# Mirrored weight rows gathered ahead of x instead of behind its first tiles, with the first layer's schedule ranked anew

## The chip, the cores and the metric

The kernel runs on one core of one Trainium2 chip. The metric is the device time of one execution in microseconds (us), the median of three runs. In the text PE is TensorE, ACT is ScalarE, DVE is VectorE, POOL is GpSimd, and SP is SyncE, which here only issues DMA transfers. The core has 16 DMA engines. Tiles of x are counted from t = 0 to 15; each holds 128 rows of 448 numbers.

## The reference

Two layers, each a spectral filter followed by a feed-forward block, on x of 2048 rows by 448 columns in bf16. The reference, cut to what is computed:

```python
def _A_ref(x, w_r, w_i):                 # spectral filter
    X = jnp.fft.rfft2(x.astype(jnp.float32), axes=(-2, -1))
    X = X * (w_r + 1j * w_i)             # w_r, w_i: 2048 x 225
    return jnp.fft.irfft2(X, s=(S, D), axes=(-2, -1)).astype(jnp.bfloat16)

def _B_ref(x, w1, b1, w2, b2):           # feed-forward, 448 -> 1792 -> 448
    h = jnp.einsum("bsd,df->bsf", x, w1) + b1
    r = jnp.where(h > 0, h, 0)
    return jnp.einsum("bsf,fd->bsd", r * r, w2) + b2

x = A_x
x = x + _A_ref(_layernorm(x), A_w_r, A_w_i)
x = x + _B_ref(_layernorm(x), B_w1, B_b1, B_w2, B_b2)
x = x + _A_ref(_layernorm(x), A_w_r, A_w_i)     # the same weights again
x = x + _B_ref(_layernorm(x), B_w1, B_b1, B_w2, B_b2)
```

## The kernel before

The Fourier transforms are matmuls with constant matrices. The stages of the first layer, in order: A1 (layer-norm statistics of each x tile, then 5 matmuls per tile against the matrix FA scaled by the tile's 1/sigma, then an eviction to XA), TD (matmuls with TD_sb), B (with G_sb), W (the product with the weights, on DVE), Bi (with H_sb), TI and AI (the way back, and the sum with x), then the feed-forward block. The second layer has the same stages with A2 in place of A1.

The W stage needs the weights in two SBUF tiles, Wa and Wb, which lie in the memory of `xin` and `yT` (the profile uses these names). Both hold rows of w_r and w_i in straight order, and the same rows once more in mirrored order. The straight rows are plain loads. For the mirrored rows of Wa, POOL issues two indirect DMA transfers (one for w_r, one for w_i), each of which gathers 64 rows of 3600 numbers by the row numbers in `back`. The mirrored rows of Wb are copied from Wa by SP, from SBUF to SBUF. Two further copies put the mirrored rows into DRAM (`Wrev`), from which the second layer reloads them.

All instructions are recorded first; a list scheduler in the kernel then orders them on each engine by a rank (`PR`, one number for each group of work) and may choose the engine of some of them from a set (`EN`). Each engine then runs its instructions in that order and waits on semaphores. The start of the recorded program:

```python
back = sb("back", [64, 1], mybir.dt.int32)
sch.add("pool", lambda e: e.iota(back[:], [[0, 1]], base=127, channel_multiplier=-2), [], [back[:]], cost=100.0)
memset(warm[:, 0:1], 1.0)
memset(epst[:, 0:1], EPS)
act(warm[:, 0:1], warm[:, 0:1], ACT.Sqrt)
sch.chain = {}                              # from here on each issuing engine keeps its DMA order
dma("act", FA_sb[:], dc["FA"])
dma("act", b1r, B_b1.rearrange("(f p) -> f p", p=P))
dma("act", J_sb[:], dc["J"])                # reversed identity
for e, a, b in (("sp", 0, 2), ("sp", 2, 4), ("sp", 4, 8), ("sp", 8, 12), ("sp", 12, 16)):
    dma(e, x_sb[:, a:b, :], x_dram[:, a:b, :], slow=1.5)
for i in range(2):                          # the gathers: they read back AND a piece of x
    o = Wa[1 - i::2, 17 * WC + 1:33 * WC + 1]
    src = A_w_i if i else A_w_r
    sch.add("pool", lambda e, o=o, src=src: e.indirect_dma_start(
        o, None, src.rearrange("(q k) l -> q (k l)", k=16), bass.IndirectOffsetOnAxis(back[:, 0:1], 0)),
        [back[:], x_sb[:, 1, 0:2]], [o], is_dma=True, cost=1200.0, lat=2.0 * 64 * 16 * WC / sch.DMA_RATE)
# ... memset of ones and of Z (on POOL)
for a, b in ((0, 2), (2, 4), (4, 6), (6, 8), (8, 10), (10, 12), (12, 14), (14, 16)):
    at[:] = 0, a // 2
    evac(xr[:, a:b, :], x_sb[:, a:b, D - 1:HD - 1:-1], "A1x")    # mirrored half of two x tiles
dma("sp", TD_sb[:], dc["TD"])

def load_W(W, f, p0, p1, first):
    # ... straight rows of w_r and w_i into W, two plain loads on SP
    for i in range(2):
        # ...
        if not first:
            dma("sp", o, Wrev[i][...], reads=[f"Wrev{i}"])       # second layer: from DRAM
        elif f:
            dma("sp", o, Wa[1 - i::2, c0:c1], slow=1.3)          # Wb: SBUF copy from Wa

for n, (p0, p1) in enumerate(RANGES):
    dma("sp", G_sb[...], dc["G"][...])
    load_W(Wa, 0, p0, p1, True)
    load_W(Wb, 1, p0, p1, True)
    dma("sp", H_sb[...], dc["H"][...])
for i in range(2):
    dma("sp", Wrev[i], Wa[1 - i::2, 17 * WC + 1:33 * WC + 1], writes=[f"Wrev{i}"])
# ...
def b1_columns():                           # bias b1 turned into columns: one matmul with J_sb
    q = _Tile(1)
    mm(q[lambda b: ps[:, b, 0:FB]], b1r, J_sb[0:FB, P - FB:P][:, ::-1], True, True)
    cp(b1T[:, 0:FB], q[lambda b: ps[:, b, 0:FB]])               # on DVE
# ...
for q in range(8):                          # stage A1
    ln_stats([2 * q, 2 * q + 1], True)      # BN_STATS on DVE; for t = 1, 3, 11 sums on ACT
    ln_rstd([2 * q, 2 * q + 1])
    first_A(2 * q)                          # scale FA into Fs, 5 matmuls, eviction to XA
    first_A(2 * q + 1)
b1_columns()
spectral(True)
ffn(False)
```

Where PE would be idle the scheduler puts matmuls on a tile of ones whose result nobody reads (line 1157, `ps<-ones`); they keep the array busy.

Of the kernel before, what the change touches and what calls it, by code (L numbers as in the profile page):

```python
# [25 lines left out]
WC = 225  # L26
# [85 lines left out]

PR = {'TD': [[1510607, 1492741, 1491034, 1343318, 1393964, -3615858, 1398823, 973064, 1485741], [2520683, -882130, 2513278, 1403817, -946609, -1006157, -1079382, -1083072, 1408461]], 'B': [[1485140, 1514860, 1501477, 1399358, 1504936, -3591466, 1503956, -3590078, 961566], [2513805, -1004943, 1405526, 2514030, 1385417, -1091018, 967616, -1128168, -974908]], 'W': [[1849139, 1836802, 1884322, 1860165, 1860418, 981529, 1855478, 1880484, 986484], [258958, 196705, -32086, -31831, 199273, -68617, -58145, -231565, -289839]], 'Bi': [[992350, -3627728, -3593143, -3606899, -3606153, -3597099, -3606581, -3605094, -3596021], [-1103789, 969189, -981009, 1254540, 970491, 1105225, 1552262, 1255862, 1105109]], 'ln': [[991126, 1016681, 13698, -12192, 3592, -9275, 58717, 59319, 60173], [-215928, -161644, -233516, -1278285, -1243220, -1249248, -1270637, -1075997, -1090994]], 'TI': [[4661211, 3603451, 3461865, -3320802, 3581733, -3314912, 3577378, -3303437, -3557233], [1148985, 1261825, -1055731, -1010406, -1074609, -1083367, -1026469, -1043258, -1050048]], 'AI': [[3603697, 4997207, 4997530, 4979074, 3482668, 4986081, 4943161, 4901552, 4992029], [-1080862, 1269571, 943460, -1102619, 1036527, 1203915, -1142225, 1214879, 1183541]], 'xb': [[966, 109389, -75965, -110358, -218149, -39133, -137679, -133462, -146632], [-874934, -227306, -1248899, -1550879, -1543334, -1550645, -1548009, -1575947, -1598280]], 'h': [[4994138, 5003910, 4900585, 4903100, 4901125, 4954442, 5002645], [-1085930, 1201108, 1202903, 1171062, 1082119, 1231856, 1056057]], 'o': [[5025464, 5043598, 4946662, 4825629, 4947511, 4769147, 4931712, 4939797, 4905816, 4965852, 4907640, 4758088, 4928290, 3664542, 4936102, 3571000], [1035960, 1041613, 1046935, 1054242, 1080488, 1155787, 1169102, 1155870, 1000585, 1239792, 1159813, 1159789, 1170072, 1159974, 1163403, 1047019]], 'A2': [[-34871, -450185, -573944, -145705, 153605, 80879, -602905, 81580, 79768, -84049, 81902, 81224, 99503, 452346, 464311, 452106]], 'A1': [[1811154, 1811355, 1842735, 1845662, 1842065, 1842576, 1826448, 1840939]], 'aux': [[1505401, -292702, -154625, 1848161]], 'A1x': [[1811802, 1797921, 1830263, 1787522, 1758506, 1787869, 1798665, 1812907]], 'A1f': [[1815437, 1814986, 1840060, 1843242, 1984370, 1791775, 1844072, 74669]], 'A1m': [[1502233, 1479272, 1517675, 1507165, 1503516, 1518961, 1518966, 1489731]], 'A1e': [[928729, 1815500, 1902353, 928717, 1675923, 1716716, 1675936, 1943634]], 'A2f': [[-34049, -127990, -606838, -439476, -138011, 89305, -571804, 80322, 86631, 80269, 450792, 462862, 54580, 466206, 59337, 450170]], 'A2s': [[480058, 130187, 326278, 591247, -431528, 73495, -83424, -22736, -590315, -851545, -746374, -585928, -115865, -441429, 129400, 466571]], 'A2m': [[4922555, 4746350, 4716000, 4727107, 4938752, 4935914, 4721112, 4719912, 3545281, -1102588, 3449906, 3544553, -1101765, 4721131, 3545586, -1101726]], 'A2e': [[43630, 40194, -682618, -204383, 162475, -55941, 457346, -202207, 210383, 251692, -640306, -43305, -207937, 110571, 278833, 493288]], 'TDe': [[954306, 1843647, 965927, 1000070, 978035, 876912, 1001412, 997131, 1721659], [234287, 1417255, 495995, 497071, -692296, -708408, 116793, 481473, -31496]], 'Be': [[1746203, 1001954, 1683907, 960405, 1780546, 967818, 1669193, 1684490, 963029], [-673471, -562228, -700927, 509333, -668554, 482845, -571588, -638456, -610624]], 'Ws': [[1889039, 1798939, 1854874, 1886651, 814650, 911035, 1938936, 1878593, 1822359], [212971, -52164, -46639, -245211, -58995, -232137, -245502, -184844, -32998]], 'Bie': [[971134, 947163, 1784532, 1001939, 1002073, 987816, 1001937, 1001943, 1001461], [1425225, 487576, -647465, -980124, -655085, -74395, -74265, -181695, -980116]], 'TIe': [[913909, 919877, 722393, -268012, 716509, -288603, 853646, 1008636, 792915], [-149289, -168051, -87569, -1092127, -1364282, -1052619, -148265, -1019412, -75009]], 'AIf': [[-308433, 3579, -182406, 12653, 80551, 7729, -143107, -148725, -142263], [-1045428, -423729, -1430802, -276728, -1103758, -1170272, -918535, -1355679, -1095738]], 'AIs': [[1037824, 921138, 43475, 988, 25617, -29947, -110980, 57417, 53976], [-160854, -145123, -793906, -883581, -1371555, -217899, -1046764, -1245627, -1325531]], 'lnq': [[254432, -546412, 123603, 7472, -193124, -186442, 9410, 836140, -149412], [-287651, -1394001, -1546005, -1125253, -1199492, -1202077, -101648, -1538229, -1522243]], 'lny': [[168910, 899305, 37852, 73400, -12667, 102790, 55869, -23759, 84279], [-244523, -464919, -208553, -1628453, -1450315, -1200119, -1077933, -1545496, -1133605]], 'fl': [[4991518, -3553909, 5045833, 5074410, 3443910, -3419830, 4794596, -3248326, 4963895], [-1100203, -1109390, -1282316, -1178605, -1592271, -1453810, 732254, -1093079, -1088719]], 'fle': [[-189687, 766990, -622264, 878315, -707948, 922239, -284319, -762173, -301700], [-1435726, -776655, -779325, -884711, -359745, -150713, -909732, -337434, -263372]], 'hA': [[-173623, -61538, 82981, 166072, -461795, 94451, 17384], [-59738, -1239374, -1219139, -169082, -1225583, -1223164, -59731]], 'hD': [[24938, -128082, -607193, -606364, -517680, 4299, -81566], [-949150, -1571960, -1533320, -1506174, -1592396, -1567483, -1293058]], 'oD': [[6213, -23599, -603373, -443574, 151235, 130944, 83824, 118459, -119914, 133726, 132035, -4922, 78773, 479772, 77491, 442182], [-1549288, -1077336, -1522386, -1421216, -1499943, -906811, -859800, -1465910, -1534119, -1026687, -1633193, -1551677, -1535519, -1571610, -1461819, -1620002]]}
EN = {'lny': ['addbdbadb', 'aadbdadbb'], 'A1x': ['brxprrdr'], 'A1f': ['xrpxprbp'], 'A1e': ['abbbbaab'], 'A2s': ['dbbabbabadbbbddb'], 'A2e': ['abaabababdaadbaa'], 'TDe': ['adbbababb', 'abadaaaad'], 'Be': ['bbbabbbaa', 'abaaabaaa'], 'Bie': ['baaaadaab', 'aaaaabbda'], 'TIe': ['adbbbbaaa', 'aabdabbbb'], 'fle': ['badababdb', 'bddaabaab']}
ENG = {"a": ("act",), "d": ("dve",), "p": ("pool",), "b": ("act", "dve"), "q": ("act", "pool"), "r": ("dve", "pool"),
       "x": ("act", "dve", "pool")}
LOOK = {"act": 0.0, "dve": 50.0, "pe": 0.0}
# [386 lines left out]
def bass_interleave_layers__spectral_gfnet__dense_activation_squared_relu__prompt_kernel(nc, A_x, A_w_r, A_w_i, B_x, B_w1, B_b1, B_w2, B_b2, out):  # L506
# [4 lines left out]
    sch = _Sched()  # L511

    with ExitStack() as es:
# [8 lines left out]
        x_sb = x_raw[:, 0:NT * D].rearrange("p (t d) -> p t d", t=NT)  # L522
# [7 lines left out]
        xb = arena[:, 2 * FB * 512:2 * FB * 512 + NT * D].rearrange("p (t d) -> p t d", t=NT)  # L530
# [7 lines left out]
        Wa = xin[:].rearrange("p t d -> p (t d)")[:, 0:33 * WC + 1]  # L538
# [76 lines left out]
        def rank(k, L=None, n=None):  # L615
            if L is not None:
                at[:] = L, n
            sch.bias = PR[k][at[0]][at[1]]

        def evac(o, i, key):  # L620
            engs = ENG[EN[key][at[0]][at[1]]]
            rank(key)
# [35 lines left out]
        def memset(o, v, eng="dve"):  # L658
            sch.add(eng, lambda e: e.memset(o, v), [], [o], cost=_free(o) / 1.92 + 60.0)  # L659
# [6 lines left out]
        out_dram = out.rearrange("b (p t) d -> p (b t) d", t=NT)  # L666
        back = sb("back", [64, 1], mybir.dt.int32)
        sch.add("pool", lambda e: e.iota(back[:], [[0, 1]], base=127, channel_multiplier=-2), [], [back[:]], cost=100.0)
        memset(warm[:, 0:1], 1.0)
        memset(epst[:, 0:1], EPS)  # L670
        act(warm[:, 0:1], warm[:, 0:1], ACT.Sqrt)
# [3 lines left out]
        dma("act", J_sb[:], dc["J"])  # L675
        for e, a, b in (("sp", 0, 2), ("sp", 2, 4), ("sp", 4, 8), ("sp", 8, 12), ("sp", 12, 16)):
            dma(e, x_sb[:, a:b, :], x_dram[:, a:b, :], slow=1.5)
        for i in range(2):
            o = Wa[1 - i::2, 17 * WC + 1:33 * WC + 1]
            src = A_w_i if i else A_w_r  # L680
            sch.add("pool", lambda e, o=o, src=src: e.indirect_dma_start(
                o, None, src.rearrange("(q k) l -> q (k l)", k=16), bass.IndirectOffsetOnAxis(back[:, 0:1], 0)),
                [back[:], x_sb[:, 1, 0:2]], [o], is_dma=True, cost=1200.0, lat=2.0 * 64 * 16 * WC / sch.DMA_RATE)
        w_dram = [w.rearrange("(q k) l -> q (k l)", k=32) for w in (A_w_r, A_w_i)]
        Wrev = nc.dram_tensor("Wrev", (2, 64, 16 * WC), BF16, kind="Internal").ap()
        memset(ones[:], 1.0)
# [554 lines left out]
```

## Time and profile before

| what | value |
|---|---|
| time, median of 3 runs | 270.92 us (270.76 to 271.03) |
| span of the profiled execution | 269.0 us |
| PE busy | 257.3 us (96%), of it 17.1 us in 54 matmuls on ones |
| DVE, ACT, POOL busy | 202.7, 184.6, 11.0 us |
| DMA | 23.25 MB; of it 0.92 MB in the POOL queue (the gathers) |
| granted TensorE clock, mean | 1.000 |

The page of the profile has a row of digits for each engine, one for each fortieth of the span (6.7 us), which is the busy share in tenths. Its chain of work follows back from the last instruction to whatever released each one, and so names what the end hung on. The lists of waits say which engine sat idle until what. A DMA instruction in the timeline shows only its issue; the time to landing is listed apart.

### The profile page before, as it was taken

The page shows a single profiled execution, that of the slowest core. Times are in us where ns is not written, and L with a number is a line of the kernel's source. Part 1 is how long each engine was busy: PE and PEld are TensorE (multiplying, and loading weights), DVE is VectorE, ACT ScalarE, POOL GpSimd, SP SyncE. Part 2 cuts the span into 40 slices and gives each one's busy share as a digit, 9 for nine tenths or more (in the row PEclk, how much of TensorE's full clock was granted, in tenths as well). Part 3 has the DMA queues.
Part 4 walks back from the last instruction along what each step waited for, and adds up shares of the span by engine and source line. Part 5 has one row for each costly group of instructions (what it writes and reads, how often), then busy time and mean ns, then how long its engine had stood idle before and what let it go on. Part 6 is the DMA issues. An engine that isn't in the chain of part 4 may idle for free.

```text
span 269.0 us, 6410 instructions
## 1 busy us (share of the span) xinstructions
PE 257.3 (96%) x2383; PEld 163.9 (61%) x2383; DVE 202.7 (75%) x704; ACT 184.6 (69%) x392; POOL 11.0 (4%) x24
## 2 busy tenths in 40 slices
PE   4899999999999999999999999998999999999996
PEld 1477997785755554444567986776754544554454
DVE  0784998999999998556599899799899855213622
ACT  4397997995889368783387998877989785005700
POOL 4361000000000000000000000000000000000000
PEclk9999999999999999999999999999999999999999
DMA  6999990003733730004000000002056200010011
GB/s 195 407 347 369 356 340 8 0 2 92 137 130 98 131 125 0 2 0 141 0 2 0 2 1 2 4 0 41 20 109 132 47 0 20 34 53 19 0 37 51
DMA packets 24474, 23.25 MB, mean 86 GB/s; under 512 B 16284, under 2 KB 20988, under 8 KB 24316
## 3 DMA queue, kind: packets, MB, share of 16 engines
q1 hardware_dynamic: 23968, 21.82, 27.3%
q0 software_dynamic: 160, 0.92, 0.8%
q8 instruction: 19, 0.31, 0.5%
q10 hardware_dynamic: 316, 0.10, 0.2%
q14 instruction: 11, 0.09, 0.1%
HBM read 15.49 MB, written 2.76 MB: 68 GB/s over the span
## 4 chain that ended last, share of the span: by engine, by line
PE 79%; ACT 10%; DVE 5%; DMA 4%; issue 1%; ACTq 0%
PE ps L588 77%; ACT XA L628 3%; ACT arena L628 3%; DMA J_sb<-c_J 2%; DMA yT<-xin 2%; PE ps L1157 2%; ACT tmp L628 1%; DVE arena L646 1%; ACT mv L611 1%; DVE x_raw L936 1%; DVE st L966 1%; ACT VT L628 1%; DVE tmp L629 0%; ACTq L583 0%; DVE x_raw L938 0%
## 5 line engine op out<-in xcount | busy, mean ns | idle before, releaser
L611 ACT ACTIVATE arena<-ps,b1T 128x512 bf16<-128x512 f32 (+1 forms) x140 | 74.0, 614 | 31.2 <-PE ps L588 30.9
L588 PE MATMUL ps<-yT,W_sb 64*128 64x512 bf16 (+1 forms) x980 | 87.1, 333 | 1.0 <-DMA yT<-xin 0.7
L588 PE MATMUL ps<-W_sb,arena 128*128 128x448 bf16 (+1 forms) x476 | 86.8, 342 | 0.0
L588 PEld LDWEIGHTS ps<-yT,W_sb 64*128 64x128 bf16 x980 | 50.3, 94 | 37.3 <-ACT arena L611 5.1
L588 PEld LDWEIGHTS ps<-W_sb,arena 128*128 128x128 bf16 x476 | 46.1, 98 | 37.8 <-DVE arena L646 0.8
L646 DVE TENSOR_TENSOR arena<-arena 128x512 bf16<-128x512 bf16 (+1 forms) x140 | 47.9, 367 | 19.1 <-ACT arena L611 18.7
L1055 DVE TENSOR_TENSOR x_raw<-ps,arena 128x448 bf16<-128x448 f32 (+1 forms) x23 | 13.3, 579 | 20.8 <-PE ps L588 20.8
L628 ACT ACTIVATE arena<-ps 128x896 bf16<-128x896 f32 (+1 forms) x32 | 25.6, 905 | 2.5 <-PE ps L588 2.5
L1157 PE MATMUL ps<-ones 128*128 128x512 bf16 x54 | 17.1, 440 | 1.1 <-DVE ones L659 1.1
L628 ACT ACTIVATE VT<-ps 128x512 bf16<-128x512 f32 x28 | 16.2, 680 | 2.7 <-PE ps L588 2.7
L628 ACT ACTIVATE XA<-ps 128x512 bf16<-128x512 f32 x30 | 16.3, 595 | 2.6 <-PE ps L588 2.4
L646 DVE TENSOR_TENSOR arena<-tmp 128x896 bf16<-128x896 bf16 (+1 forms) x32 | 17.1, 591 | 0.3
L738 ACT ACTIVATE tmp<-x_raw 128x448 bf16<-128x448 bf16 x14 | 8.0, 574 | 13.4 <-DVE x_raw L1051 13.3
L588 PE MATMUL ps<-H_sb,arena 128*128 128x128 bf16 x256 | 16.5, 219 | 0.5 <-DVE arena L646 0.5
L738 ACT ACTIVATE VT<-x_raw 128x448 bf16<-128x448 bf16 x24 | 13.8, 582 | 4.3 <-DVE x_raw L938 4.3
L588 PEld LDWEIGHTS ps<-H_sb,arena 128*128 128x128 bf16 x256 | 14.8, 98 | 2.5 <-DVE arena L646 2.5
L646 DVE TENSOR_TENSOR tmp<-VT 128x224 bf16<-128x224 bf16 (+1 forms) x56 | 16.2, 318 | 0.2
L938 DVE SCALAR_TENSOR_TENSOR x_raw<-ps,x_raw 128x448 bf16<-128x448 f32 x24 | 14.3, 616 | 0.8 <-PE ps L588 0.8
L588 PE MATMUL ps<-arena,G_sb 128*128 128x224 bf16 x128 | 14.3, 259 | 0.1
L628 ACT ACTIVATE tmp<-ps 128x896 bf16<-128x896 f32 (+1 forms) x16 | 12.7, 853 | 1.9 <-PE ps L588 1.9
L611 ACT ACTIVATE mv<-mv,epst 128x2 f32<-128x2 f32 (+1 forms) x31 | 9.1, 300 | 5.6 <-DVE mv L752 4.4
L588 PEld LDWEIGHTS ps<-arena,G_sb 128*128 128x128 bf16 x128 | 11.9, 98 | 0.7 <-ACT arena L628 0.6
(77 smaller groups left out, 266.2 us busy)
## 6 DMA issues: line engine op xcount, KB each, us to landing
W_sb<-in_B_w_dram SPq DMA_DIRECT2D x2, 896.0 KB, 6.5
out_dram<-x_raw SPq DMA_DIRECT2D x15, 112.0 KB, 1.7
W_sb<-in_B_w_dram SPq DMA_DIRECT2D x1, 1568.0 KB, 12.7
x_raw<-in_A_x_dram SPq DMA_DIRECT2D x3, 448.0 KB, 6.2
H_sb<-c_H SPq DMA_DIRECT2D x1, 1088.0 KB, 9.3
yT<-xin SPq DMA_DIRECT2D x4, 225.0 KB, 5.3
Wrev<-xin SPq DMA_DIRECT2D x2, 450.0 KB, 10.4
xin<-Wrev SPq DMA_DIRECT2D x4, 225.0 KB, 3.8
```

The costliest lines, as they stand in the source:

```text
L588: op = sch.add("pe", lambda e: e.matmul(_res(o), lhsT, rhs, start=start, stop=stop, skip_group_check=skip), [lhsT, rhs], [o], cost=max(_fr ...
L611: sch.add("act", lambda e: e.activation(o, _res(i), func, **kw), rd, [o], cost=c)
L628: op = sch.add("act", lambda e: e.activation(o, _res(i), ACT.Copy) if h[0].eng == "act" else e.tensor_copy(o, _res(i)), [i], [o], cost=c[" ...
L646: sch.add(eng, lambda e: e.tensor_tensor(o, _res(a), b, op), [a, b], [o], cost=_free(o) / rate + 69.0)
L738: sch.add("act", lambda e: e.activation(o, x, ACT.Square, accum_out=sd[:, t, 1:2]), [x], [o, sd[:, t, 1:2]], cost=560.0)
L936: sch.add("dve", lambda e, xx=xx, xi=xi, r=r: e.tensor_tensor(xx, _res(r), xi, ALU.add), [r, xi], [xx], cost=536.0)
L938: small(lambda e, xx=xx, xi=xi, r=r, i=i: e.scalar_tensor_tensor(out=xx, in0=_res(r), scalar=1.0, in1=xi, op0=ALU.mult, op1=ALU.add, accum ...
L966: small(lambda e, i=i: e.bn_stats(st[:, i, 0:6], x_sb[:, i, 0:D]), [x_sb[:, i, 0:D]], [st[:, i, 0:6]], 536.0)
L1055: sch.add("dve", lambda e: e.tensor_tensor(o, _res(i), xb[:, t, d0:d1], ALU.add), [i, xb[:, t, d0:d1]], [o], cost=(d1 - d0) / 0.96 + 69.0)
L1157: return lambda e: e.matmul(ps[:, b, :], ones[:], ones[:, None, :].to_broadcast([P, 4, P]), start=True, stop=True)
```

## The change

The two gathers are recorded before everything else that moves data, directly behind the `iota` that writes their row numbers, and they no longer read x. In the kernel before they named a piece of x as an input, and so waited until its first two tiles had landed. The purpose is to have the mirrored rows of Wa in SBUF sooner: SP's queue waits for them before it copies them into Wb and issues all later loads. All transfers stay the same in number, size and issuing engine.

Beside it the ranks of the first layer and the engine sets of some evictions and copies were fitted anew; those of the second layer (the second list of each entry) are unchanged. In the sets, a is ACT, d DVE, p POOL, b ACT or DVE, q ACT or POOL, r DVE or POOL, x any of the three; the letters of A1x are one for each pair of x tiles.

```diff
-PR = {'TD': [[1510607, 1492741, ... ], [2520683, -882130, ...]], ... }        # cut
-EN = {'lny': ['addbdbadb', 'aadbdadbb'], 'A1x': ['brxprrdr'], 'A1f': ['xrpxprbp'], 'A1e': ['abbbbaab'], 'A2s': ['dbbabbabadbbbddb'], ... }
+PR = {'TD': [[1288052, 1208402, ... ], [2520683, -882130, ...]], ... }        # cut
+EN = {'lny': ['dadddbbaa', 'aadbdadbb'], 'A1x': ['bxrqqbqp'], 'A1f': ['qxrpqxdp'], 'A1e': ['bbadabaa'], 'A2s': ['bbdabbbdbaadbddd'], ... }
@@ -666,6 +666,12 @@
         sch.add("pool", lambda e: e.iota(back[:], [[0, 1]], base=127, channel_multiplier=-2), [], [back[:]], cost=100.0)
+        for i in range(2):
+            o = Wa[1 - i::2, 17 * WC + 1:33 * WC + 1]
+            src = A_w_i if i else A_w_r
+            sch.add("pool", lambda e, o=o, src=src: e.indirect_dma_start(
+                o, None, src.rearrange("(q k) l -> q (k l)", k=16), bass.IndirectOffsetOnAxis(back[:, 0:1], 0)),
+                [back[:]], [o], is_dma=True, cost=1200.0, lat=2.0 * 64 * 16 * WC / sch.DMA_RATE)
         memset(warm[:, 0:1], 1.0)
@@ -675,12 +681,6 @@
             dma(e, x_sb[:, a:b, :], x_dram[:, a:b, :], slow=1.5)
-        for i in range(2):
-            o = Wa[1 - i::2, 17 * WC + 1:33 * WC + 1]
-            src = A_w_i if i else A_w_r
-            sch.add("pool", lambda e, o=o, src=src: e.indirect_dma_start(
-                o, None, src.rearrange("(q k) l -> q (k l)", k=16), bass.IndirectOffsetOnAxis(back[:, 0:1], 0)),
-                [back[:], x_sb[:, 1, 0:2]], [o], is_dma=True, cost=1200.0, lat=2.0 * 64 * 16 * WC / sch.DMA_RATE)
         w_dram = [w.rearrange("(q k) l -> q (k l)", k=32) for w in (A_w_r, A_w_i)]
```

In the built program this changes the order on the engines as follows. POOL issues both gathers right behind its memset and ahead of its first copy of x. On PE the warm-up matmuls on ones become 6, then 9 behind the bias matmul (they were 6 and 7), and 7 behind the first four tiles (they were 8). On DVE the bias copy stays the first instruction that waits. Of the 8 mirrored copies of x, DVE makes none (it made 2), ACT 2 (0), POOL 6 (6). Of the 16 scalings of FA, DVE makes 3 (5), ACT 4 (1), POOL 9 (10). Of the 16 evictions to XA, DVE makes 3 (0) and ACT 13 (16). In the first layer's TD, B and Bi stages some blocks of matmuls swap places, and so do some blocks of the second layer's A2. The order of the second layer's other matmuls is the same.

## The prediction

> **What bounds the kernel now.** I read the row of digits for the whole span first, then the chain of work that ended last in order of time, then the waits of the first 60 us, then the DMA queues slice by slice for the first 14 us. The row of PE:
>
> ```profile
> PE   4899999999999999999999999998999999999996
> ```
>
> PE stands at 9 tenths or more nearly everywhere except in the first two fortieths. The chain says the same in pieces (start, length, what):
>
> ```profile
> 1.86 5.50 DMA J_sb<-c_J
> 7.66 3.10 PE ps L1157 x7
> 10.76 2.92 PE ps L588 x15
> ...
> 21.42 2.56 ACT XA L628 x5
> 24.07 16.54 PE ps L588 x200
> ...
> 54.24 89.96 PE ps L588 x784
> ```
>
> From 24.07 us on the chain is mostly PE matmuls, and between 54.24 and 144.2 nothing else. Before 24.07 it is something else: the landing of the reversed identity J_sb at 7.36, then warm-up matmuls on ones, then stage A1, which ends with five ACT evictions to XA. So this change can act on the time through one door: the moment at which A1 ends, 24.07 us, and after it whatever the newly ranked order does. The waits of the first 60 us (who waited for what: us in total, times, longest) and, in the second fence, those of SP's queue:
>
> ```profile
> DVE b1T L650 <- PE ps L588: 6.7, 1, 6.7
> PE ps L588 <- DMA J_sb<-c_J: 3.6, 1, 3.6
> POOL xin L681 <- DMA x_raw<-in_A_x_dram: 2.7, 1, 2.7
> ```
>
> ```profile
> SPq L583 <- DMA xin<-in_A_w_r_dram,back: 4.4, 1, 4.4
> ```
>
> DVE's first real instruction is the bias copy b1T; it waits for the bias matmul, and that for J_sb. Though x[0:2] lands at about 3.6 us (ACT's first sum starts at 3.64), DVE starts its statistics only at 7.79. The last two lines are the waits that the change removes: POOL's 2.7 us for x, and SP's 4.4 us (7.2 to 11.62) for the first gather. The question is whether somebody needs what SP issues afterwards. The first user is the W stage on DVE:
>
> ```profile
> 27.23 0.39 DVE L646 TENSOR_TENSOR tmp<-arena,xin 128x448 bf16<-128x448 bf16 x1
> 27.54 0.38 DVE L646 TENSOR_TENSOR tmp<-arena,yT 128x448 bf16<-128x448 bf16 x1
> ```
>
> It starts at 27.23 directly behind the evictions of stage B, with no wait for a DMA, 12 us or more after the gathers: issued at 4.54 and 6.38, they landed after 7.1 and 6.7 us, at 11.6 and 13.1. From 27.23 to 45.8 DVE has no idle time at all. So the removed waits stand on nobody's path.
>
> **What the skill says.** The page "DMA: Bandwidth & Descriptors", section "Issuing engines are not separate DMA queues", says that transfers issued from SP, ACT and GpSimd run on the same 16 DMA engines and interleave; its section "Queues, rings and completion order" says that each engine goes round-robin between the queues that have work, one packet at a time. The trace agrees. In the slice from 9 to 10 us, with the gathers (q0) under way, the queues show
>
> ```profile
> q0 software_dynamic: 38, 0.27, 65.0%
> q1 hardware_dynamic: 83, 0.16, 42.4%
> ```
>
> (packets, MB, share of 16 engines), while SP's queue q1 had 97.8% in the slice from 7 to 8. A gather packet takes 0.65 x 16 / 38 = 0.274 us. So gathers push the loads of other queues back by what they move. The page "TensorE: Matmul & The Clock Gate", section "Part 1: The HAM clock gate", says that the array runs at half rate until it has been busy for some 3.4 us. The trace has the two rates (matmuls on ones at a pitch of 0.43 us at 8 us and of 0.22 at 14), though the change comes at about 13, some 5.4 us after PE restarted at 7.49. So a warm-up matmul is dear early and cheap later.
>
> **The change part by part.**
>
> *Removed: POOL's wait for x.* Worth nothing by itself. POOL's next needed result is a scaled FA at 11.55, behind 4.3 us of idle time.
>
> *Removed: SP's stall.* Nothing on the path, as shown. The DMA engines weren't idle during the stall either: their share was 0.97 in both slices from 5 to 15 us, since SP had queued 2.6 us of issues ahead. Only 14 to 16 us dips (0.88, 244 GB/s), worth perhaps 0.7 us of transfer, ahead of a W stage with slack.
>
> *Moved: 0.92 MB of gather traffic into the loading of x, FA and J_sb.* The first gather can be issued when POOL's memset ends, at 1.84 us, the second about 1.1 later. In the kernel before the first q0 packet appears in the slice from 8 to 9 us, at about 8.8, some 4.3 us behind the issue at 4.54. The same lag puts it at about 6.2 now. At 400 GB/s the gathers take 2.3 us of all 16 engines, so loads that are still queued at 6.2 (the last two of x, TD, G, straight rows) land up to 2.3 us later. The last piece of x was issued at 2.6 and landed 6.8 us later, at 9.4; now about 11.5. DVE reaches those tiles only at about 17 us, so that is hidden. TD_sb, issued at 3.07 with 8.1 us to landing, goes from 11.2 to 13.5 and is needed at 24. Hidden as well.
>
> *J_sb is the one load with no slack.* Its packets and those behind it in ACT's queue (q10) number 37, 66 and 41 in the slices from 4 to 5, 5 to 6 and 6 to 7 us, none later. Those after 6.2, some 33, are 2 for each engine. If each waits for one gather packet more, J_sb is 2 x 0.274 = 0.55 us late; if the first q0 packet comes at 5.2 it is 1.5 us, and if at 7, nothing. I take 0.3 us. It goes straight into the start of DVE and PE.
>
> *The new order in A1.* Three sums. First, PE has two more cold matmuls on ones behind the bias matmul: 2 x 0.43 = 0.86 us, first tile not before 11.5 (was 10.65); but now all four of the first tiles' scaled FA are made at once, so the four groups end at about 11.5 + 7 x 0.21 + 13 x 0.11 = 14.4 against 14.04, or 0.4 later. Second, ACT from its first square root behind the four evictions (14.74) to the last XA (23.97) had no idle time: 6 square roots at 0.19, two sums at 0.65, one FA at 0.4, 12 evictions at 0.53, together 9.2 us. Now it has the same roots and sums, one copy of x at 0.5, two FA at 0.8 in all and 9 evictions at 4.8: 8.5 us, 0.7 less. Third, DVE takes three evictions at about 0.65 behind its last reciprocal (21.45 before, then idle from 22.3 to 25.42): it would end them at about 23.7 + 0.3. The two engines thus end A1 at nearly the same time as before, shifted by J_sb: 24.07 + 0.3, give or take 0.8.
>
> *From 24 us on.* Number and shape of all matmuls are unchanged. PE had no gap of its own from 24.07 to 40.45 and from 54.24 to 144.2, so swapping blocks there moves nothing unless it makes a wait. The filler counts of the program behind A1 are equal (2, 5, 2, 2, 3, 3, 1, 3, 6, 2, 2, 1, 1), so the scheduler expects the same gaps. I put 0 here with an uncertainty of 0.8 us, from the latency-bound stretches 40.45 to 54.2 and 144 to 187, where PE works 40.3 of 43.0 us.
>
> Sum: 270.9 + 0.3 (J_sb) + 0 (A1's order) + 0 (later order), and a little for waits that a rank fitted to a model does not see: 271.3 us.
>
> **Rivals.** (a) *A real gain:* the mirrored rows are early, all loads come earlier, and the time falls by some of SP's 4.4 us, to about 268. Against it: no instruction of the W stage waited for a DMA. For it only that the A1 order relieves ACT, worth at most 0.7 us: 270.2. (b) *x and J_sb are starved:* the gathers start at 5 us or earlier, J_sb lands 1.5 to 2.5 us late, and DVE, PE and ACT start A1 that much later: 272.5 to 273.5. For it: DVE's order still has the bias copy ahead of all statistics. Against it: the 4.3 us lag. (c) *The new ranks miss in a later stage,* A2 above all, whose engine sets changed: a gap of 1 us on PE inside 54 to 144 where there was none: 272.3. Nothing in the profile of before can show it. (d) *It is hidden anyway,* both ways: 270.9.
>
> **Range and chances.** The terms of half a microsecond to 0.8 combine to about 1.1 us, and (b) is longer than (a), so 270.0 to 272.9 should hold it 8 times in 10. Two per cent is 5.4 us. No path to 5.4 us less exists, since only 24 us lie ahead of PE's work; 5.4 more needs (b) and (c) together at their worst. So: faster 0.02, same 0.95, slower 0.03. That the time is above 270.9 rather than below I hold at about two to one.
>
> **What would show each step.** J_sb's time to landing was 5.5 us; I expect 5.5 to 6.5, and DVE's first BN_STATS at 7.8 to 8.8. First q0 packets at 5.5 to 7 us. SP's wait for the gather gone or below 2 us, with the W stage still waiting for no DMA. First tile's matmul at 11.3 to 12, start of TD at 23.8 to 25, and the shift of TD against 24.07 found again at the end, within 1 us. The prediction is wrong in its reasons if TD starts on time and the end moves, for then the ranks behind A1 do it; or if TD starts early because loads were what A1 or W waited for.

## The result: 273.48 us, 1% slower

| | before | changed kernel |
|---|---|---|
| time, median | 270.84 us (270.2 to 271.03) | 273.48 us (273.04 to 274.02) |
| ratio to the kernel before, 95% interval | | 1.0103 (1.0078 to 1.0127) |
| span of the profiled execution | 269.0 us | 271.6 us |

The predicted time was 271.3 us and the range ended at 272.9. The time lies 0.6 us above the range, inside the 2% that were called most likely. A second timing of the same kernel (run e12, below) gave 273.23 us and 1.0116 (1.0068 to 1.0164).

### Where the 2.6 us of the profiled pair are

Four marks of PE cut both executions into stages (us):

| | before | after | growth of the stage that ends here |
|---|---|---|---|
| bias matmul (J_sb has landed) | 7.49 | 8.80 | +1.31 |
| first matmul of A1 | 10.65 | 12.71 | +0.75 |
| first matmul of TD | 24.07 | 26.12 | -0.01 |
| first matmul of the feed-forward block (yT, W_sb) | 54.22 | 56.27 | 0.00 |
| first matmul behind it, in layer 2 (TQ_sb) | 147.73 | 150.26 | +0.48 |
| end | 269.0 | 271.6 | +0.07 |

The waits of the first 60 us of the changed kernel, PE and DVE, and then those of SP's queue (who waited for what: us in total, times, longest):

```profile
DVE b1T L650 <- PE ps L588: 8.0, 1, 8.0
PE ps L588 <- DMA J_sb<-c_J: 5.0, 1, 5.0
```

```profile
SPq L583 <- DMA xin<-in_A_w_r_dram,back: 2.5, 1, 2.5
SPq L583 <- DMA xin<-in_A_w_i_dram,back: 1.3, 1, 1.3
```

POOL's wait for x ahead of the gathers is gone. SP still waits for the two gathers, 2.5 and 1.3 us instead of the 4.4 and 1.0 of the kernel before, and nobody misses it: the W stage begins two microseconds later than before (29.28 instead of 27.23), and again behind the evictions of stage B, with no wait for a DMA in brackets. The timeline of DVE in the changed kernel (start, length, what):

```profile
28.62 0.62 DVE L629 CAST arena<-ps 128x448 bf16<-128x448 f32 x1
29.28 0.39 DVE L646 TENSOR_TENSOR tmp<-arena,xin 128x448 bf16<-128x448 bf16 x1
```

What grew ahead of A1 is PE's wait for J_sb (3.6 to 5.0 us) and DVE's wait behind it (6.7 to 8.0). The queues in the slice from 6 to 7 us of the changed kernel show why J_sb could be late (packets, MB, share of 16 engines):

```profile
q1 hardware_dynamic: 74, 0.24, 65.2%
q0 software_dynamic: 16, 0.12, 31.0%
q10 hardware_dynamic: 33, 0.01, 3.5%
```

The gather packets (q0) now run beside 33 packets of ACT's queue (q10), to which J_sb belongs, and 10 more of that queue follow in the next two slices. Before, q10 had nothing left at 7 us, and the first gather packet came at about 8.9 us, when J_sb had landed.

A1 as a whole took 13.4 us in both profiles, and that equality misleads. PE's timeline in the kernel before, in A1, only those lines that had a wait ahead of them (the last bracket: idle time, and what ended it):

```profile
16.12 0.27 PE L588 MATMUL ps<-Fs,x_raw 128*128 128x256 bf16 x1 [0.19 <-ACT Fs L639]
...
22.07 0.28 PE L588 MATMUL ps<-Fs,x_raw 128*128 128x256 bf16 x1 [0.17 <-DVE Fs L640]
...
24.07 2.08 PE L588 MATMUL ps<-TD_sb,XA 128*128 128x224 bf16 x20 [0.30 <-ACT XA L628]
```

and in the changed kernel:

```profile
17.11 0.27 PE L588 MATMUL ps<-Fs,x_raw 128*128 128x256 bf16 x1 [0.23 <-POOL Fs L640]
...
18.59 0.27 PE L588 MATMUL ps<-Fs,x_raw 128*128 128x256 bf16 x1 [0.23 <-ACT XA L628]
...
21.12 0.28 PE L588 MATMUL ps<-Fs,x_raw 128*128 128x256 bf16 x1 [0.18 <-ACT Fs L639]
...
22.89 0.27 PE L588 MATMUL ps<-Fs,x_raw 128*128 128x256 bf16 x1 [0.51 <-DVE Fs L640]
...
26.12 1.31 PE L588 MATMUL ps<-TD_sb,XA 128*128 128x224 bf16 x12 [0.45 <-ACT XA L628]
```

Three waits with 0.66 us have become five with 1.60. That A1 took no longer all the same comes from something that the change did not do: in the profile of before the A1 matmuls ran at half rate (0.21 us apart) for their first 2.5 us, in that of after for 0.6. Those runs below in which the array happened to be fast from the start show the difference free of this.

The last loss lies in the feed-forward block. The chain of the changed kernel has a DMA inside the stretch that was pure PE before:

```profile
70.43 3.28 DMA yT<-xin
73.76 72.99 PE ps L588 x552
```

### The profile page after: what moved, and what is told of

Its sections match the earlier page's. It is cut to its first block, busy times and chain, and to the rows that moved or that the text cites. A ratio compares the mean times of both kernels' runs of the same rounds, so it can differ in the third digit from the quotient of the medians.

```text
span 271.6 us, 6414 instructions
## 1 busy us (share of the span) xinstructions
PE 257.2 (95%) x2384; PEld 163.0 (60%) x2384; DVE 205.0 (75%) x707; ACT 184.4 (68%) x390; POOL 10.5 (4%) x23
## 4 chain that ended last, share of the span: by engine, by line
PE 62%; DVE 13%; ACT 5%; DMA 3%; issue 1%; DVEq 0%
PE ps L588 62%; DMA yT<-xin 3%; ACT arena L628 3%; DVE arena L646 3%; DVE x_raw L936 2%; DVE st L966 2%; DVE x_raw L938 1%; DVE tmp L646 1%; DVE xin L655 1%; ACT XA L628 1%; DVE VT L646 1%; ACT VT L628 1%; DVE tmp L629 0%; DVE x_raw L1055 0%; DVE rstd L774 0%
## 5 line engine op out<-in xcount | busy, mean ns | idle before, releaser
L588 PEld LDWEIGHTS ps<-yT,W_sb 64*128 64x128 bf16 x980 | 49.5, 94 | 38.8 <-ACT arena L611 4.8
L628 ACT ACTIVATE XA<-ps 128x512 bf16<-128x512 f32 x26 | 14.6, 592 | 9.2 <-PE ps L588 9.2
L1157 PE MATMUL ps<-ones 128*128 128x512 bf16 x55 | 17.7, 447 | 1.1 <-DVE ones L659 1.1
L646 DVE TENSOR_TENSOR arena<-tmp 128x896 bf16<-128x896 bf16 (+1 forms) x32 | 17.1, 590 | 0.3
```

Of the source, the lines that this page charges most:

```text
L588: op = sch.add("pe", lambda e: e.matmul(_res(o), lhsT, rhs, start=start, stop=stop, skip_group_check=skip), [lhsT, rhs], [o], cost=max(_fr ...
L628: op = sch.add("act", lambda e: e.activation(o, _res(i), ACT.Copy) if h[0].eng == "act" else e.tensor_copy(o, _res(i)), [i], [o], cost=c[" ...
L646: sch.add(eng, lambda e: e.tensor_tensor(o, _res(a), b, op), [a, b], [o], cost=_free(o) / rate + 69.0)
L1157: return lambda e: e.matmul(ps[:, b, :], ones[:], ones[:, None, :].to_broadcast([P, 4, P]), start=True, stop=True)
```

## The experiments

All runs compute the whole reference. "Order" means the sequence of instructions on every engine; several edits work on the ordered lists, after the scheduler and before the code is emitted, so that nothing else moves. Each ratio is to the kernel before, run alongside. "Stretch" is the feed-forward stretch, from the first yT, W_sb matmul to the first TQ_sb matmul. Statistics start 0.30 us after the bias matmul wherever J_sb holds them.

### Gathers and order taken apart: e1, e2

e1 is the changed kernel's order, with the wait for x put back:

```diff
+        xload = [op for op in sch.ops["sp"] if op.is_dma][0]
+        for op in sch.ops["pool"]:
+            if op.is_dma:
+                op.deps.append(xload)
```

> The changed kernel with its order of instructions kept exactly, and only the gathers' wait for the first two tiles of x put back. Theory J (early gather packets push the load of J_sb back, and DVE and PE start behind it): J_sb lands 5.5 us after its issue instead of 6.8, DVE's first statistics start at 7.8 instead of 9.1, TD starts 1.3 us sooner than in the changed kernel (24.8 instead of 26.1), and the time is about 272.2 us. Rival O (the newly ranked order makes the whole loss): J_sb moves but the time stays at 273.5. Rival D (everything is the gathers' traffic): the time goes back to 270.9.

e2 is the kernel before, with both gathers moved up and their wait removed:

```diff
+        g = [op for op in pool if op.is_dma]
+        for op in g:
+            op.deps = [d for d in op.deps if d.eng != "sp"]
+            pool.remove(op)
+        pool[2:2] = g
```

> The kernel before with its order on PE, ACT, DVE and SP kept exactly; only the two gathers are issued by POOL behind its memset, ahead of x, without the wait. Theory J: J_sb takes 6.8 us to land instead of 5.5, DVE's statistics start at 9.1, TD starts at 25.4 instead of 24.1, the time is about 272.2 us. Rival O: the time stays at 270.9. Rival D: about 273.5.

e1: 272.56 us, 1.0077 (1.006 to 1.0094). e2: 271.27 us, 1.0034 (1.0018 to 1.005). So with 270.4 us beside them the new order alone costs 2.1 us (1.6 to 2.5), the early gathers alone 0.9 (0.5 to 1.35). The changed kernel has both, 2.8 us at 1.0103: they add up. Most of the loss is the order, which the prediction had put at zero.

### What carries the gathers' cost: e10, e11, e12

e10 issues the gathers ahead of POOL's memset, at 1.61 instead of 2.02 us; e12 is the changed kernel once more; e11 has the early gathers in a kernel in which nothing early waits for J_sb (e8, below).

```diff
-        pool[2:2] = g          # e2
+        pool[1:1] = g          # e10, on the changed kernel
```

> The changed kernel, with the two gathers issued ahead of POOL's 0.94 us memset instead of behind it; nothing else is moved. Theory J: the gathers' first packets come about 1 us sooner, at about 5.2 us, J_sb's remaining packets meet twice as many of them, J_sb lands 7.3 to 8 us after its issue (6.8 in the changed kernel, 5.5 to 6.0 without early gathers), DVE starts at 9.6 to 10.3, and the time is 274 to 274.5. Rival (the delay of J_sb was chance and not the gathers): J_sb lands after 5.5 to 6.8 us as before and the time stays at or below 273.5.

> The changed kernel itself, beside the three others on one chip. With it the share of the gathers can be read without the new order: about 2.7 us over the kernel before, J_sb landing 6.5 to 7 us after its issue if early gathers regularly delay it; if that was chance, 5.5 to 6.

> The kernel before with the bias matmul behind A1 (265.7 us in its own run), and on top of it the gathers issued ahead of x as in the change; the order on PE, ACT, DVE and SP is kept exactly. Theory J (early gathers hurt only through J_sb, which nothing early waits for here): DVE starts at 3.7 us as without early gathers, and the time is the same within 0.3 us, 265.4 to 266.0. Rival X (the gathers also push x back, and A1, now four microseconds sooner, runs into the late tiles): a wait for x of 0.5 to 2 us appears on DVE or POOL and the time is 266.2 to 267.7.

e10: 273.62 us, 1.0131 (1.0092 to 1.0169). e12: 1.0116. Earlier gathers are not resolved from the changed kernel. In both, J_sb landed sooner than theory J had it, 6.5 us after its issue in e10 (7.3 to 8 expected) and 5.7 in e12 (6.5 to 7): by what was put down beforehand these two landings speak for chance. e11: 266.11 us, 0.9849 (0.9817 to 0.9882), against e8's 0.9848 (0.982 to 0.9876) without early gathers, and TD starts at 19.19 us in both. Their trace shows no cost of the gathers once J_sb is off the path, though the two intervals would leave room for a microsecond.

The direct proof is missing. The bias matmul's start scatters from run to run: 7.02 to 8.20 us, mean 7.74, in the ten profiles with late gathers where J_sb held it (before, e1, e5, e6, e7, e9, e13 to e16), and 7.55, 7.71, 8.54 and 8.80, mean 8.15, in the four with early ones (e2, e12, e10, after). The difference of 0.4 us has the right sign and the predicted size (0.3), but the scatter is as large. Some packets of q10 were also left at 7 us with late gathers, 4 in e1 and 8 in e16 against 10 in after. In e2's own profile J_sb landed after 5.5 us, as before, and that execution was the fastest of its seven (269.81 us).

### Whether J_sb starts A1: e3, e4, e8

e3 (on the changed kernel) and e4 (on the kernel before) exchange J_sb and FA_sb in ACT's queue; e8 makes the bias matmul, and so DVE's copy of it, wait for the end of A1.

```diff
-dma("act", FA_sb[:], dc["FA"])
-dma("act", b1r, ...)
-dma("act", J_sb[:], dc["J"])
+dma("act", J_sb[:], dc["J"])            # e3, e4
+dma("act", b1r, ...)
+dma("act", FA_sb[:], dc["FA"])
```

```diff
-    mm(q[...], b1r, J_sb[...], True, True)
+    # e8: the same matmul, with the XA columns of the last tile named as one more input
+    sch.add("pe", lambda e: e.matmul(...), [b1r, J_sb[...], XA[:, :, :, :, 60:64]], [...], ...)
```

> The changed kernel, but ACT issues J_sb first and FA last of its three loads; all other orders are kept. Theory J: J_sb lands at about 3.3 us, ahead of the gathers' first packets, DVE starts with x[0:2] at about 3.7 instead of 9.1, and A1 ends earlier by 2 to 4 us, held by the last pieces of x or by FA, which is now behind the gathers: 270 to 271.5 us. If the gathers hurt A1 through x rather than through J_sb, DVE starts early and then waits for x, and the time falls by less than 1 us, to 272.5 or more.

> The kernel before, but ACT issues J_sb first and FA last of its three loads; all other orders are kept. Theory J: J_sb lands at about 3.3 us, DVE starts its statistics at about 3.7 instead of 7.8, TD starts at 20.5 to 22 instead of 24.1, the time is 267.5 to 269.5 us. Rival (A1 is bound by x's arrival or by ACT's evictions whatever DVE does): 270.3 to 270.9.

> The kernel before, with the bias matmul and its copy on DVE made to come after the last eviction of A1, so that nothing early waits for J_sb any more. Theory J (the landing of J_sb starts DVE, and FA lands early): DVE starts statistics at about 3.7 us instead of 7.8, first tile's matmul at about 6.7 instead of 10.7, TD at about 20 instead of 24.1, the time about 266.7 us. Rival (the end of A1 is then held by the arrival of x or the cold TensorE clock): TD at 22 to 23, 268.5 to 270.

e4: 268.6 us, 0.9929 (0.9888 to 0.9969). e3: 272.01 us, 1.0059 (1.0043 to 1.0076). J_sb now lands 2.3 to 2.5 us after its issue and DVE starts at 4.1, but FA_sb, last in the queue, takes J_sb's old place (6.2 us to landing in e4, 7.2 in e3) and PE waits 1.95 us in e4 and 3.30 in e3 for the first scaled FA. So e4 gained what was expected, and e3, at 272.01, missed its 270 to 271.5. e8: 265.66 us, 0.9848 (0.982 to 0.9876), by the ratio 4.1 us less than the kernel before, and with e11 the fastest of all. DVE's timeline in the kernel before and, behind it, in e8:

```profile
7.70 0.17 DVE L650 COPY b1T<-ps 128x14 f32<-128x14 f32 x1 [6.65 <-PE ps L588]
7.79 0.62 DVE L758 BATCH_NORM_STATS2 st<-x_raw 128x6 f32<-128x448 bf16 x1
```

```profile
3.67 0.63 DVE L759 BATCH_NORM_STATS2 st<-x_raw 128x6 f32<-128x448 bf16 x1 [2.63 <-DMA x_raw<-in_A_x_dram]
...
18.60 0.17 DVE L650 COPY b1T<-ps 128x14 f32<-128x14 f32 x1 [1.17 <-PE ps L734]
```

The statistics now start when x is there, 4.1 us sooner, and TD at 19.19 instead of 24.07 (about 1 us of this is the faster array of e8's profile, whose A1 took 12.30 us). So it was not x that held the start of A1, but the first waiting instruction in DVE's queue, and that waited for a 32 KB load which no statistic needs. This is the door through which early gathers can act.

### The order in A1: e5, e7, e9

e5 takes two of the nine matmuls on ones behind the bias matmul out of e1. e7 gives A1 the ranks and engine sets of the kernel before, with the gathers behind x, and leaves everything else new (the old ranks all lowered by one number, so that A1 stays ahead of the rest). e9 gives each of the 16 tiles its own buffer for the scaled FA (there are six, used in turn), and so removes the waits for a buffer from e1.

```diff
+        fill = [i for i, op in enumerate(pe) if op.unit is None]      # e5
+        for i in (fill[14], fill[13]):
+            del pe[i]
```

```diff
+for k in ('A1', 'A1x', 'A1f', 'A1m', 'A1e'):                        # e7
+    PR[k], EN[k] = those of the kernel before
```

```diff
-            f = Fs[:, t % NFS, :]                                     # e9
+            f = F16[:, t, :]
```

> The changed kernel with the gathers' wait for x put back, and only two of the nine matmuls on ones behind the bias matmul taken out. Theory F (the longer filler holds the first tiles of A1): the first tile's matmul comes 3.3 us after the landing of J_sb instead of 3.9, and the time falls by 0.4 to 0.6 us against the same kernel with nine, to about 272.1. Rival: A1 is held later, by a ring of waits between ACT, DVE and PE around tiles 10 and 11; then the first tiles come sooner but TD does not, and the time stays at 272.5.

> The kernel before (gathers behind x), with the new ranks and engine sets everywhere except in stage A1, which keeps those of before. Theory (the new order costs twice, about 1.2 us in A1 and about 0.9 us in the first feed-forward block): TD starts 15.7 to 16.7 us behind the landing of J_sb as in the kernel before, the stretch from the first feed-forward matmul to the first TQ matmul is 94.4 us instead of 93.5, and the time is about 271.3 us, 0.9 over before. Rival (the order's loss is all in A1): 270.4. Rival (all behind A1): 272.4.

> The changed kernel with the gathers' wait for x put back, its order of instructions kept exactly, and the scaled FA of each of the 16 tiles in a buffer of its own instead of a ring of six, so that no scaling in A1 waits any more for PE to release a buffer. Theory R (in the new order the ring closes a circle: the late tiles 10 and 11 on PE hold buffers, the scalings on DVE and POOL wait for PE, and PE for them): the waits of the scalings for PE (3.0 us on POOL, 0.5 on DVE) vanish and the stretch from DVE's first statistics to TD shrinks by 0.5 to 1.0 us against the same kernel with the ring, to about 15.8 at an early TensorE warm-up; time about 271.8. Rival S (the late tiles themselves hold A1, through ACT's sums for tile 11, the square root and the scaling in one chain; the ring waits are only their shadow): the ring waits vanish and TD comes when it did, 16.6 us at an early warm-up, time 272.5.

| run | A1's order | bias matmul to first A1 matmul | first A1 matmul to TD | half rate in A1 for | PE's waits in A1 |
|---|---|---|---|---|---|
| e2, e7, e13 | old | 3.16, 3.16, 3.15 | 12.38, 12.29, 12.37 | 0.4, 0, 0.4 | 0.66 |
| e1, e12, e16 | new | 3.78, 3.73, 3.91 | 13.10, 13.11, 13.28 | 0, 0, 0.4 | 1.6 |
| before | old | 3.16 | 13.42 | 2.5 | 0.66 |
| e5 | new, 7 fillers | 3.51 | 14.34 | 2.5 | 1.6 |
| e9 | new, own buffers | 3.91 | 13.25 | 1.7 | 1.1 |

With the array fast from the start, the new order takes 0.6 to 0.7 us more up to the first A1 matmul and 0.8 from there to TD, 1.4 together. Of the first part, e5 shows that the two added fillers are worth 0.2 to 0.4; without them PE still starts 0.35 us later than in the old order, for it waits for the first scaled FA (0.25 us for ACT). e5's time, 272.63 us and 1.011 (1.0079 to 1.014), is no better. The second part is PE's waits, 0.95 us more, less one matmul on ones (0.2 us) of which the new order has seven and not eight behind the first tiles. e5 against before, both with 2.5 us at half rate, is again 0.9 longer.

e9 took the wait for DVE's scaling (0.51 us) away. PE's waits fell to 1.1 us, all of A1 to what e16 has although its array was 1.3 us later. Its 271.9 us, 1.0058 (1.0041 to 1.0075), are 0.5 us below e1 by the ratios, which the intervals do not resolve. e7: 271.63 us, 1.0073 (1.0046 to 1.01). Its A1 is back at the old length, and yet it is no faster than e1: its stretch in the feed-forward block was 95.20 us, against 93.51 before and 94.47 in e1.

### The order in the feed-forward block: e6, e13

The ranks pull the normalisation of tile 3 of the feed-forward input (DVE, `xin`) apart from that of tile 2; three squarings lie between. In the kernel before, one line holds both:

```profile
60.29 0.73 DVE L655 TENSOR_SCALAR xin<-x_raw,mv,rstd 128x512 bf16<-128x512 bf16 x2
```

in e7 there are two lines, with a microsecond from one to the other:

```profile
59.76 0.41 DVE L655 TENSOR_SCALAR xin<-x_raw,mv,rstd 128x512 bf16<-128x512 bf16 x1
60.79 0.41 DVE L655 TENSOR_SCALAR xin<-x_raw,mv,rstd 128x512 bf16<-128x512 bf16 x1
```

SP's first DMA transpose of `xin` into yT in this block stands behind the later of the two; it was issued 6.87 us after the block began in the kernel before, and 7.79 in e7, e1 and after. e6 puts tile 3's normalisation directly behind tile 2's in e1; e13 does the same in e7.

```diff
+        a, b = norm[2], norm[3]                 # DVE's normalisations into xin, in order
+        dve.remove(b)
+        dve.insert(dve.index(a) + 1, b)
```

> The changed kernel with the gathers' wait for x put back, and only one DVE instruction moved: in the first feed-forward block the normalisation of tile 3 stands directly behind that of tile 2 instead of three instructions later. Theory T (the new ranks pull this pair apart, the first DMA transpose comes later, SP's queue hands the delay on, and PE waits for the transposes of tiles 4 to 7): the first transpose is issued 0.6 us sooner against the start of the block, PE's wait for yT falls from 1.0 us to below 0.4, and the stretch from the first feed-forward matmul to the second layer's first TQ matmul falls from 94.5 us to about 93.9; the time to about 272.0. Rival: the wait is set by SP's interleaved weight loads, not by this pair; the stretch stays at 94.5.

> Stage A1 ordered as in the kernel before, gathers behind x as before, everything else ranked as in the changed kernel, and tile 3's normalisation in the feed-forward block put directly behind tile 2's. Theory (the feed-forward loss comes from that normalisation, which makes a transpose late): from the first statistics to TD 15.2 us, the feed-forward stretch 93.7 instead of 95.2 in the same kernel without the move, PE's wait for the transposed tile below 0.3 us, the time 0.7 to 1.5 us below that kernel's 1.0073, so 1.002 to 1.005. Rival (the other reordered blocks of the feed-forward stage cost the time): the stretch stays above 94.5 and the ratio at 1.007.

The waits from 50 to 140 us, e7 and, behind it, e1 (the kernel before has no wait for yT):

```profile
PEld ps L588 <- DMA yT<-xin: 2.1, 2, 1.3
PE ps L588 <- DMA yT<-xin: 1.4, 2, 0.9
```

```profile
PEld ps L588 <- DMA yT<-xin: 1.0, 1, 1.0
PE ps L588 <- DMA yT<-xin: 0.7, 1, 0.7
```

e6, in which e1's waits have shrunk to

```profile
PEld ps L588 <- DMA yT<-xin: 0.2, 1, 0.2
```

and in e13 no wait for yT is left. The stretch went from 94.47 to 93.73 us (e1 to e6) and from 95.20 to 93.58 (e7 to e13). Not all of either is the moved instruction: the nine profiles with the order of e1 in this block range from 93.99 (after) to 94.51 us (e3), and in e7's profile the first transpose took 4.7 us to land instead of 3.1 (before, e1, e13), which makes 0.9 of its 1.4 us of PE's waits. Why it landed late, the runs do not show. The times: e6 271.89 us, 1.0087 (1.0051 to 1.0122), too wide to tell; e13 270.74 us, 1.0013 (0.9997 to 1.003), with e7 at 1.0073. e13 is the changed kernel's order everywhere but in A1 and at one instruction, and within the 0.8 us of its interval it is as fast as the kernel before. So, as far as these times resolve it, the whole loss of the order is A1 and this one normalisation.

### Which link of A1: e14, e15, e16

e14 is e1 with tile 11's last three small statistics operations moved up on DVE, and the reciprocal behind them, in front of one BN_STATS each. e15 is e14, e9 and e6 in one; e16 is e1 again, as the mark beside them.

```diff
+        dve[i:i] = [rec]            # reciprocal of tiles 10 and 11 ahead of a BN_STATS
+        dve[j:j] = trip             # mean, square and variance of tile 11 ahead of an earlier BN_STATS
```

> The changed kernel's order with the gathers waiting for x, and on DVE the three small operations that finish tile 11's statistics put ahead of one statistics instruction more, and the reciprocal of tiles 10 and 11 ahead of one more. Theory (the chain from those statistics over ACT's square root and scaling to PE is a link of A1's loss): ACT's waits of 0.44 and 0.31 us before the root and the scaling go below 0.15 each, PE's wait of 0.46 us for tile 10's scaled FA goes, from the first statistics to TD 16.1 instead of 16.5 us at a similar warm-up, the time 0.3 to 0.5 us below that of the same order without the move. Rival (PE is held by the scalings after it, on DVE): the waits move to tile 12 and TD stays at 16.5 us.

> The same as the run before it, and beside it a buffer of its own for each tile's scaled FA and tile 3's normalisation moved behind tile 2's. Theory (three separate chains make the new order's loss: late statistics, ring waits, late transpose): from the first statistics to TD 15.6 us, the feed-forward stretch 93.7, the ratio 1.000 to 1.003. Rival (the loss of A1 lies in the work itself, more of it per engine, and not in these waits): from the first statistics to TD still 16.3 or more and the ratio 1.005 or more.

> The changed kernel's order with the gathers waiting for x once more, unchanged, as the mark for the runs beside it: 1.0077 again, give or take 0.0015; from the first statistics to TD 16.5 us, or 17.0 or more if TensorE goes to full rate late; the feed-forward stretch 94.4.

e16: 272.89 us, 1.0078 (1.005 to 1.0107), as e1. e14: 274.24 us, 1.0125 (1.0086 to 1.0163). e15: 272.25 us, 1.0057 (1.0037 to 1.0078). The theory fell. PE's timeline in e14:

```profile
20.48 0.27 PE L588 MATMUL ps<-Fs,x_raw 128*128 128x256 bf16 x1 [0.51 <-POOL Fs L640]
...
23.66 0.27 PE L588 MATMUL ps<-Fs,x_raw 128*128 128x256 bf16 x1 [0.84 <-DVE Fs L640]
```

The wait for ACT's scaling is gone, and a longer one for POOL's stands in its place; the reciprocal of the pair before now comes behind the operations that were moved up, and ACT waits 0.55 us for it. PE's waits in A1 rose to 2.26 us (and in this profile its array was at half rate for the first 2.1 us of A1). In e15 the stretch is 93.58 us as expected, but from the statistics to TD it took 17.1 us and not 15.6: PE waits 0.51 us for POOL's scaling where it waited for ACT's, 0.19 instead of 0.51 for DVE's, and the sum of its waits is 1.61 us as in e1; the array was at half rate for the first 0.8 us of A1 besides. The rival put down for e15, that the loss lies in more work for the engines and not in these waits, met both of its marks (16.3 us or more, 1.005 or more), though the late array has a part in the first. The profiles give it some ground: from the first statistics to TD, DVE is busy for 13.2 us in e1 and e12 and for 12.3 in e2 and e7. What these runs do not settle is which link, or which work, would have to move to give the 0.8 us back. In e14 and e15 a wait taken from one of the three engines that scale FA came back at another; in e9 it did not.

## Why the prediction was wrong

**Removed waits.** Right. Neither POOL's wait nor SP's stood on the path. The prediction expected SP's 4.4 us to fall below 2; 2.5 were left, beside 1.3 for the second gather, and that too changed nothing.

**Gathers against J_sb.** The mechanism named fits but isn't proven, and the first q0 packets came at 6 to 7 us as worked out from the lag. The Trainium skill's page "DMA: Bandwidth & Descriptors", section "Queues, rings and completion order", has the engines go round-robin between the queues; the slice above shows the three queues sharing the engines, and no run here shows the order of their turns. The page counts a turn as a packet of typically 9 to 17 descriptors; the estimate took it as one packet of the trace, and whether the two are the same isn't shown. The size was too small: 0.3 us predicted, 0.9 (0.5 to 1.35) in the time of e2, where the estimate's own upper end was 1.5. The profile of after shows 1.3, more than the cost that the times give. Part of that is the scatter of J_sb, which the prediction did not have: it read one landing time, 5.5 us, as a constant. In the second profile of the changed kernel (e12) J_sb landed after 5.7 us, the statistics began at 8.00, the first tile's matmul at 11.44 and TD at 24.55, all inside the ranges given; in the first it was 6.8, 9.10, 12.71 and 26.12, all outside. That e12's TD fell into its range is in part luck: its array was fast from the start of A1, while the 24.07 from which the range was built holds some 1.0 us of half rate (13.42 us for A1 against 12.38 in e2).

**The new order in A1, "0, give or take 0.8".** This is the first step that failed. It compared what ACT, DVE and PE have to do in A1, found two sums nearly equal, and let the engines pack that work without gaps. ACT's work did fall (12.3 us busy in e2 from the first statistics to TD, 12.0 in e12, where a fall of 0.7 stood), but DVE's, of which only the three evictions were counted, grew from 12.3 to 13.2. What made the stage longer is, first, PE's waiting for the other engines, 0.66 to 1.6 us; how far DVE's added work and how far the order of the operations makes these waits stays open. Second, PE's start. It was computed about right: the first tile 0.6 to 0.7 us later where 0.86 stood, and the matmuls on ones behind the fourth tile 0.4 us later, as computed (5.91 us after the bias matmul in e12, 5.51 in e2). But the sum then went by ACT and DVE alone and let this be absorbed. Together 1.4 us, not 0.

**From 24 us on, "0".** This is the second. Equal filler counts were taken to mean equal gaps. Up to the feed-forward block that held: 30.15 us from TD to its first matmul in both profiles. Inside it, rival (c) came true, in the feed-forward block and not in A2: 0.48 us in the profiled pair, 1.0 in e1, 1.7 in e7. PE's 90 us without a gap of its own said that PE was always fed, and not how closely: with the first transpose issued 0.9 us later (7.79 instead of 6.87 us into the block), PE waits for one that SP issues behind it, 0.7 us in e1.

**The sum.** The mistakes all had the same sign: order +2.1, gathers +0.9, together 3.0 by the single runs and 2.6 to 3.1 measured, where +0.4 stood. The range added its terms as if they were independent and centred on zero. "Two to one for slower" was right, and so was within 2%. The 272.5 to 273.5 of rival (b) holds the measured time by luck, for the gathers make only a third of the loss.

## What to carry to other kernels

Look first at the head of each in-order queue: one early instruction that waits for a small late load holds everything behind it, and here to move it was worth 4.1 us, more than the whole change. When an order changes, two nearly equal busy sums don't promise an equal stage: sum the work of every helper, list the waits of the critical engine with their releasers, before and after, and reckon with a wait removed at one helper coming back at another. And split a change that carries both an edit and a new schedule: here the idea cost 0.9 us and the schedule fitted to it 2.1.

## What was not expected of the hardware

*When TensorE reaches full rate.* The page "TensorE: Matmul & The Clock Gate", section "Part 1: The HAM clock gate", gives about 3.4 us of activity, counted in a window that runs freely, so that the moment varies from run to run. Counted from the bias matmul, it was at most 3.2 us in e7, about 4.7 in e15, 5.7 before (the prediction read 5.4) and 6.0 in e5. Where the order on PE up to there is the same (e1, e12, e16 and e9) the A1 matmuls still ran at half rate for 0, 0, 0.4 and 1.7 us. In the old order this is worth a microsecond: 13.42 us for A1 in the profile of before, 12.29 to 12.38 in e2, e7 and e13. What decides it, these runs do not show, nor the window itself. The granted clock of the profile doesn't tell either: from the first statistics to TD it stands at 1.00 in the kernel before, with the 2.5 us of half rate inside, and at 0.89 in e2.

*Landing of a small load behind large ones.* J_sb, 32 KB, issued at 1.86 us, let its matmul start at 7.02 to 8.20 us with late gathers, a scatter of 1.2 us with nothing changed ahead of it in the queues. A single profile of such a load is one draw.
